# Attention with normalised q and k: q's first transfer is issued by ScalarE before its first table load instead of after it

## The chip, the cores and the metric

The kernel runs on one core of one Trainium2 chip. The core has five engines that work side by side, each with its own list of instructions: TensorE (PE in the profile; PEld is its weight load), VectorE (DVE), ScalarE (ACT), GpSimd (POOL) and SyncE (SP, which here only issues transfers). SP and ACT both issue DMAs; each engine that issues has a queue of its own, and all queues are served by the same 16 DMA engines. Engines wait for each other, and for transfers, on semaphores. The metric is the device time of one launch in microseconds (us); lower is better.

## The reference

For each of 32 heads, with 2048 positions of 20 numbers each in bf16, the rows of q and k are divided by their norms (plus 1e-6), the logits are scaled by one number `t` per head, and softmax attention is formed:

```
qn = q / (jnp.sqrt((q * q).sum(axis=-1, keepdims=True)) + eps)
kn = k / (jnp.sqrt((k * k).sum(axis=-1, keepdims=True)) + eps)
logits = jnp.einsum('bhqd,bhkd->bhqk', qn, kn) * t[None, :, None, None]
attn = _softmax(logits, axis=-1)
return jnp.einsum('bhqk,bhkd->bhqd', attn, v)
```

The inputs are q, k, v of shape 1 x 32 x 2048 x 20 and `t` of 32 numbers.

## The kernel before

The 32 heads are taken in 8 groups of 4. For a group, q and k are loaded (tile `qk`), squared (`sqs`), summed (`ssum`), turned into inverse norms (`rn`), multiplied and padded to 32 columns per head (`qpad`, `kpad`), and transposed (`qT`, `kT`). For every block of 128 keys by 512 queries PE forms logits in PSUM; their exponentials are taken in two ways. ACT takes them with its Exp table, two blocks to an instruction (line 1053, `pA` from `psA`). DVE and POOL take the other blocks by integer arithmetic on the bits of a float (lines 398 and 411, `dI` and `dS` from `psD`). PE multiplies the results with v (`vaug`), whose extra column of ones gives the softmax denominator.

No engine decides its order at run time. `make_plan` simulates the five engines with costs and latencies written in the source, and puts each operation in its engine's list when it is simulated to start; the instructions are then written out in that order with the semaphore waits that the data needs. At the start of the program some operations are placed by hand with `finish(op, start, cost, lat)`: it writes the start and the end (start plus latency) into the operation and appends it to its engine's list. The list of ACT is then sorted by start.

The start of the first group matters here. Only the first 4 of its 16 rows per partition are fetched first: the k part by SP, the q part by ACT, each 128 partitions x 4 heads x 80 numbers (80 KB), line 464. Behind k's first part SP issues `t` (tile `tb16`, line 618), the rest of k, the rest of q, and v. ACT's list starts with a dummy activation on `act_scr` (line 611) for which a table load for the square root is put in front of it; it waits for a memset on DVE (line 592). ACT squares k's first part itself (line 377), DVE squares q's (line 376) and sums both (line 378, q's first). ACT takes the two square roots (line 379), and behind the second loads the table for the exponential (line 639). DVE goes on to inverse norms (lines 380, 381, 384) and to `qpad` and `kpad` (line 389).

Between the sums and the norms DVE finds the largest `|t|` into `tmx` (line 619, the operation `flag`). The program exists in two complete plans, and every engine reads `tmx` and takes a branch (lines 1491 and 1492) to one of them. PE does so right after its first 10 warming matmuls (line 666); so its small transposing matmuls (line 677, with more warming ones of line 684 between them), which give `qT` and `kT` for the first logits, come behind the branch. The first logits are at line 849, and fillers that keep PE busy are at line 662.

Of the kernel before, what the change touches and what calls it, by code (L numbers as in the profile page):

```python
# [161 lines left out]
def bass_standalone__qk_norm__prompt_kernel(  # L162
# [15 lines left out]
    with ExitStack() as es:  # L178
# [236 lines left out]
        def part_op(hg, c):  # L415
            b = hg % 2
            f = lambda tl: tl[b][:, :, :, :].rearrange("p h r d -> p (h r d)")
            return dve("vh", NH * R * VW, R4, lambda e: e.tensor_single_scalar(f(vpart[c]), f(vaug), c, ALU.mult),
                       [("v", b, hh) for hh in range(NH)] + [("vz", b)], [("vh", b, c)])
# [29 lines left out]
        def load_qk(hg, a, part=None):  # L449
            b = hg % 2  # L450
            r0, r1 = (0, R) if part is None else PARTS[part]
            if a == 0 and hg == HG - 1:

                ops = []
                for x in range(4):
                    s_ = q[0, hg * NH:(hg + 1) * NH].rearrange("h (i x r) d -> x i h (r d)", x=4, r=R)[x]
                    d_ = qk[b][32 * x:32 * x + 32, a, :, :, :].rearrange("p h r d -> p h (r d)")
                    keys = [("qk", b, a, 0), ("qk", b, a, 1)]
                    ops.append(dma("ldq", lambda e, d=d_, s=s_: e.dma_start(d, s), keys if x else [], [("qkx", b, x)] if x else keys, 0.5, 4.0))
                return ops  # L460
            src = (q, k)[a][0, hg * NH:(hg + 1) * NH].rearrange("h (p r) d -> p h r d", p=128)[:, :, r0:r1, :]
            s_ = src.rearrange("p h r d -> p h (r d)")
            d_ = qk[b][:, a, :, r0:r1, :].rearrange("p h r d -> p h (r d)")
            return [dma("ld" + "qk"[a], lambda e: e.dma_start(d_, s_), [],
                        [("qk", b, a, i) for i in ((0, 1) if part is None else (part,))],
                        0.5, 4.0 if part != 0 else LOAD0)]
# [10 lines left out]
        def tr_op(hg, which, r0, r1):  # L477
            b = hg % 2
            pad, T = (kpad, kT) if which == "k" else (qpad, qT)
            src = pad[b][:, r0:r1, :, :].rearrange("p r h d -> p (r h d)")  # L480
            dst = T[b][:, r0 * 128:r1 * 128].rearrange("p (r n) -> p r n", n=128)
            keys = [(which + "T", b, r) for r in range(r0, r1)]
            o = dma("T" + which, lambda e: e.dma_start_transpose(dst, src),
                       [(which + "pad", b, r) for r in range(r0, r1)], keys, 0.58 + 0.17 * (r1 - r0), TRL + 0.17 * (r1 - r0) + TRK * (hg == 0 and which == "k"))
            o.info = hg
            return o
# [19 lines left out]
        def make_plan(share):  # L506
# [56 lines left out]
            def finish(op, start, cost, lat):  # L563
                op.start, op.done = start, start + lat
                P.put(op)
# [24 lines left out]
            o = P.link(Op("DVE", "z", lambda e: e.memset(zt[:, :], 0.0), [], ["zt"], 0.25, 0.3))  # L590
            finish(o, 0.15, o.cost, o.lat)
            o = P.link(Op("DVE", "z", lambda e: e.memset(act_scr[:, :], 1.0), [], ["scr"], 0.1, 0.15))
# [9 lines left out]
            for b in (1, 2, 3):  # L602
# [8 lines left out]
            o = P.link(Op("ACT", "tab", lambda e: e.activation(act_scr[:, 0:16], act_scr[:, 0:16], ACT.Sqrt),  # L611
                          ["scr"], ["scr0"], 1.5, 1.6))
# [11 lines left out]
            want_sp(load_qk(0, 1, 0)[0])  # L624
            o = P.link(load_qk(0, 0, 0)[0])
            o.eng = "ACT"
            finish(o, 0.8, o.cost, o.lat)
            P.order["ACT"].sort(key=lambda o: o.start)
            t_load()
            for a in (1, 0):  # L630
# [34 lines left out]
            o = Op("PE", "heat", None, ["zt"], [("psA", 0), ("psD", OB(0))])  # L665
# [41 lines left out]
            for r0, r1, a0, a1 in ((4, 16, 1, 2), (4, 16, 0, 1)):  # L707
# [13 lines left out]
                for w_ in ("q", "k")[a0:a1][::-1]:  # L721
                    for c0, c1 in ((8, r1) if w_ == "k" else (r0, r1),):
                        o = tr_op(0, w_, c0, c1)
# [5 lines left out]
            if share:  # L729
                for c in vpart:  # L730
                    o = part_op(0, c)
# [675 lines left out]
            while left:  # L1407
                progressed = False
                for e in P.order:
                    while pos[e] < len(P.order[e]):  # L1410
                        o = P.order[e][pos[e]]
# [29 lines left out]


        plans = [make_plan(True), make_plan(False)]
        n_flag = max(o.cnt for o in plans[0][0].order["DVE"] if o.name == "flag")
        cut = {}
# [109 lines left out]
```

## Time and profile before

| what | us |
|---|---|
| median of 3 runs | 587.89 |
| lowest and highest of them | 587.89, 589.05 |
| the profiled execution's own time | 588.97 |
| its span, first to last instruction | 587.2 |
| ACT busy in the span | 576.7 |
| PE busy in the span | 577.3 |
| DVE busy in the span | 576.1 |
| ACT's first exponential starts at | 9.81 |

Times inside the profile count from the start of the span. An instruction row has its start, its duration, the engine, the line, the operation and the tiles written and read; in square brackets stands how long the engine was idle before it and what ended that. A row with an engine's name and a q (ACTq, SPq) is the sequencer of that engine, which issues transfers; its duration is that of the issue, not of the transfer. For transfers the time "to landing" counts from the start of the issue to the last signal on the semaphore.

### The profile page before, as it was taken

Reading aid. Unit: us, or ns where it says so; the run is one execution under the profiler, and the core shown is the slowest. Engines: PE = TensorE matmul, PEld = TensorE weight load, DVE = VectorE, ACT = ScalarE, POOL = GpSimd, SP = SyncE. Lnnn points to the kernel's source line nnn. Section 1 sums busy time; section 2 is a strip of 40 time slices with the busy share of each in tenths; the row PEclk is TensorE's granted clock in tenths of the full one; section 3 lists DMA queues with packets and bytes.
Section 4 is the critical chain, followed back from the end, with each engine's and each line's share of the span. In section 5 each row is a group of like instructions: output and inputs, shape, how many; then the busy total and the mean of one; then the engine's idle time right before and its main releaser. Section 6 shows DMA issues by size and latency. Waiting matters only on the chain.

```text
span 587.2 us, 16438 instructions
## 1 busy us (share of the span) xinstructions
PE 577.3 (98%) x6799; PEld 164.4 (28%) x6799; DVE 576.1 (98%) x1040; ACT 576.7 (98%) x632; POOL 498.2 (85%) x924
## 2 busy tenths in 40 slices
PE   8999999999999999999999999999999999999997
PEld 4332222322223222232222322222222322222221
DVE  7999999999999999999999999999999999999996
ACT  6999999999999999999999999999999999999996
POOL 2587898897988899788898889888989789999995
PEclk9999999999999999999999999999999999999999
DMA  5640605205051131410523113430054401101000
GB/s 68 102 58 1 118 2 45 48 2 117 5 68 22 39 81 10 60 23 19 102 17 60 17 37 84 31 61 2 1 103 40 68 2 37 38 3 23 7 8 17
DMA packets 132144, 24.19 MB, mean 41 GB/s; under 512 B 121312, under 2 KB 132064, under 8 KB 132064
## 3 DMA queue, kind: packets, MB, share of 16 engines
q1 hardware_dynamic: 131264, 22.96, 25.5%
q8 instruction: 55, 0.90, 0.6%
q10 hardware_dynamic: 800, 0.12, 0.1%
q14 instruction: 25, 0.20, 0.1%
HBM read 7.87 MB, written 2.62 MB: 18 GB/s over the span
## 4 chain that ended last, share of the span: by engine, by line
ACT 90%; PE 6%; DVE 3%; DMA 1%; issue 0%; DVEq 0%
ACT pA L1053 90%; PE psD L871 3%; PE psA L849 2%; DMA qk<-in_q_dram 1%; DVE ssum L301 0%; DVE dI L398 0%; PE psD L849 0%; PE psA L684 0%; DVE rn L329 0%; DVE sqs L298 0%; DVE ssum L378 0%; PE psD L677 0%; DVE accT L423 0%; DVE kT L718 0%; DVE rsb L323 0%
## 5 line engine op out<-in xcount | busy, mean ns | idle before, releaser
L1053 ACT ACTIVATE pA<-psA 128x1024 f16<-128x1024 f32 (+1 forms) x624 | 572.4, 1180 | 1.3 <-PE psA L849 1.1
L411 POOL INT64_ADD dS<-dI x907 | 492.1, 558 | 69.3 <-DVE ost L438 15.7
L398 DVE TENSOR_SCALAR dI<-psD 128x512 int16<-128x512 f32 (+1 forms) x785 | 490.6, 688 | 1.0 <-PE psD L849 0.4
L849 PE MATMUL psA<-qT,kT 32*128 32x512 bf16 x1248 | 245.0, 385 | 1.9 <-ACT pA L1053 0.4
L849 PE MATMUL psD<-qT,kT 32*128 32x512 bf16 x801 | 244.5, 383 | 0.8 <-DVE dI L398 0.6
L871 PE MATMUL psD<-dS,vaug 128*22 128x512 f16 x1600 | 210.2, 383 | 0.0
L871 PE MATMUL psD<-pA,vaug 128*22 128x512 f16 (+1 forms) x1248 | 183.7, 383 | 0.1
L871 PE MATMUL psD<-dI,vaug 128*22 128x512 f16 x800 | 138.7, 383 | 0.0
L871 PE MATMUL psD<-dI,vhalf 128*22 128x512 f16 x800 | 137.6, 382 | 0.0
L849 PEld LDWEIGHTS psA<-qT,kT 32*128 32x128 bf16 x1248 | 58.6, 91 | 225.9 <-ACT pA L1053 219.7
L849 PEld LDWEIGHTS psD<-qT,kT 32*128 32x128 bf16 x801 | 60.3, 91 | 15.7 <-issue 7.5
L871 PEld LDWEIGHTS psD<-dS,vaug 128*22 128x22 bf16 x1600 | 45.5, 89 | 60.9 <-issue 34.4
L871 PEld LDWEIGHTS psD<-pA,vaug 128*22 128x22 bf16 x1248 | 40.5, 89 | 46.8 <-issue 37.9
L871 PEld LDWEIGHTS psD<-dI,vhalf 128*22 128x22 bf16 x800 | 31.0, 89 | 26.1 <-issue 18.9
L871 PEld LDWEIGHTS psD<-dI,vaug 128*22 128x22 bf16 x800 | 30.9, 89 | 23.4 <-issue 19.8
L423 DVE STREAM_TRANSPOSE accT<-psD 128x512 f32<-128x512 f32 x32 | 22.5, 705 | 2.7 <-PE psD L871 2.7
L438 DVE TENSOR_TENSOR ost<-accT,rec 128x320 bf16<-128x320 f32 x32 | 16.3, 510 | 0.0
L662 PE MATMUL psD<-zt 128*128 128x128 bf16 x130 | 12.9, 228 | 0.0
L271 DVE TENSOR_TENSOR sqs<-qk 128x1280 bf16<-128x1280 bf16 x14 | 11.7, 839 | 0.0
L805 PE MATMUL psD<-ind,sqT 128*128 128x128 bf16 x140 | 11.5, 221 | 0.0
L662 PEld LDWEIGHTS psD<-zt 128*128 128x128 bf16 x130 | 8.1, 101 | 8.4 <-issue 8.4
L805 PEld LDWEIGHTS psD<-ind,sqT 128*128 128x128 bf16 x140 | 7.9, 98 | 4.8 <-issue 3.9
(66 smaller groups left out, 87.6 us busy)
## 6 DMA issues: line engine op xcount, KB each, us to landing
vaug<-in_v_dram SPq DMA_DIRECT2D x32, 80.0 KB, 4.3
qk<-in_k_dram SPq DMA_DIRECT2D x7, 320.0 KB, 3.9
out_dram<-ost SPq DMA_DIRECT2D x28, 80.0 KB, 1.9
qk<-in_q_dram SPq DMA_DIRECT2D x6, 320.0 KB, 4.0
qk<-in_q_dram SPq DMA_DIRECT2D x4, 80.0 KB, 3.5
out_dram<-ost SPq DMA_DIRECT2D x7, 40.0 KB, 2.0
qk<-in_k_dram SPq DMA_DIRECT2D x1, 240.0 KB, 3.9
qk<-in_q_dram SPq DMA_DIRECT2D x1, 240.0 KB, 4.5
```

The costliest lines, as they stand in the source:

```text
L271: ops.append(dve("sq", w_, R2, lambda e, o=sq, x=x3: e.tensor_tensor(o, x, x, ALU.mult), [("qk", b, a, i) for i in parts] + [("qkx", b, i) ...
L398: lambda e: e.tensor_scalar(dst, psD[:, pb * QW:(pb + n) * QW], 1024.0 * LOG2E, 15360.0 - 1024.0 * LOG2K + SHIFTS[0], ALU.mult, ALU.add),
L411: lambda e: e.int64_add(o.bitcast(U64), x.bitcast(U64), add), rd, wr)
L423: return dve("drain", QW, R1, lambda e: e.transpose(accT[:, 16 * b:16 * b + 16, :].rearrange("p b d -> p (b d)"), psO_(sb)), [("psD", OB(s ...
L438: dve("omul", 320 * n, R1, lambda e: e.tensor_tensor(dst, num, rcb, ALU.mult), at + ar, [("ost", hg % 2, g) for g in range(g0, g1)]),
L662: return lambda e: e.matmul(bank, zt[:, 0:128], zt[:, 0:n], start=False, stop=False, skip_group_check=True)
L805: mms = [lambda e, g=g, j=j: e.matmul(dst, sqT[:, (5 * g + j) * 128:(5 * g + j + 1) * 128], ind[:, j, 96 - 32 * g:224 - 32 * g], start=g + ...
L849: return lambda e: e.matmul(dst, lhsT, rhs, tile_position=(32 * hh, 0))
L871: return lambda e: e.matmul(dst, lhsT, rhs, start=first, stop=last, skip_group_check=True, tile_position=(0, 32 * hh))
L1053: a = Op("ACT", "exp", lambda e, s=src, d=dst: e.activation(d, s, ACT.Exp), [("psA", slot)], [("pA", pslot, i) for i in range(WAVES[slot]) ...
```

## The change

The transfer of q's first part gets the planned start 0.0 instead of 0.8, and 0.8 more latency, so its planned end is as before. Since ACT's list is sorted by planned start and the dummy activation stands at 0.6, the transfer now comes first on ACT.

```
@@ make_plan @@
             want_sp(load_qk(0, 1, 0)[0])
             o = P.link(load_qk(0, 0, 0)[0])
             o.eng = "ACT"
-            finish(o, 0.8, o.cost, o.lat)
+            finish(o, 0.0, o.cost, o.lat + 0.8)
             P.order["ACT"].sort(key=lambda o: o.start)
             t_load()
```

This is the head of ACT's list, as a difference from before to now with the semaphore waits; `act_scr` is the dummy activation's scratch tile, and the wait for `s_dma0` is the one for k's first part:

```order
 L1516 UNCONDITIONAL_BRANCH [waits barrier_Pool_Activation_PE_DVE_SP_release]
+L464 DMA qk<-in_q_dram 128x4x80
 L611 ACT_TABLE_LOAD
 L611 ACTIVATE act_scr<-act_scr 128x16 [waits s_dve]
-L464 DMA qk<-in_q_dram 128x4x80
 L377 ACTIVATE sqs<-qk 128x320 [waits s_dma0]
 L379 ACTIVATE nr<-ssum 128x16 [waits s_dve] x2
```

The issue of q's first transfer moved up past the table load and past the dummy activation with its wait for DVE. The lists of PE, DVE, POOL and SP are the same as before, with the same waits.

More of the change, by code (lines that the diff above doesn't have):

```diff
@@ L626, in make_plan @@
             o.eng = "ACT"
-            finish(o, 0.8, o.cost, o.lat)
+            finish(o, 0.0, o.cost, o.lat + 0.8)
             P.order["ACT"].sort(key=lambda o: o.start)
```

## Prediction

> **What bounds the kernel.** I read the page's chain first, then its groups, then the chain in order of time. The page says that nearly all of the span is one chain on ACT:
>
> ```profile
> ACT pA L1053 90%; PE psD L871 3%; PE psA L849 2%; DMA qk<-in_q_dram 1%; DVE ssum L301 0%; DVE dI L398 0%; PE psD L849 0%; PE psA L684 0%; DVE rn L329 0%; DVE sqs L298 0%; DVE ssum L378 0%; PE psD L677 0%; DVE accT L423 0%; DVE kT L718 0%; DVE rsb L323 0%
> L1053 ACT ACTIVATE pA<-psA 128x1024 f16<-128x1024 f32 (+1 forms) x624 | 572.4, 1180 | 1.3 <-PE psA L849 1.1
> ```
>
> The 624 exponentials of line 1053 cover 572.4 us, and ACT has 1.3 us of idle time in front of them, 1.1 of it before the first. So the end is the start of the first exponential plus a dense stream: whatever brings that start and the stream's inputs earlier by one amount brings the end earlier by the same. The chain in order of time says what the first exponential hangs on:
>
> ```profile
> 1.28 3.46 DMA qk<-in_q_dram
> 4.76 0.34 DVE sqs L376
> ...
> 5.12 0.88 DVE ssum L378 x2
> 6.00 0.09 DVE tmx L619
> ...
> 7.13 0.50 PE psA L684 x3
> ...
> 22.95 526.43 ACT pA L1053 x574
> ```
>
> From 1.28 to 4.74 the whole program waits for q's first 80 KB. Behind it come DVE's square, sums and norms, PE's small matmuls, and at last ACT, which heads the chain from 22.95 on. Of the opening stage this transfer is by far the longest piece.
>
> **The issue, moved.** The first rows of the timeline on ACT, on SP and on DVE:
>
> ```profile
> 0.80 0.47 SPq L464 DMA_DIRECT2D qk<-in_k_dram  x1
> 0.81 1.28 ACT L611 ACT_TABLE_LOAD   x1 [0.81 <-PEq L1540]
> 1.16 0.09 DVE L592 MEMSET act_scr<- 128x32 f32 x1
> 1.28 0.46 ACTq L464 DMA_DIRECT2D qk<-in_q_dram  x1
> 1.34 0.48 SPq L618 DMA_DIRECT2D tb<-in_t_dram  x1
> 2.10 0.22 ACT L611 ACTIVATE act_scr<-act_scr 128x16 f32<-128x16 f32 x1
> 3.00 0.47 ACT L377 ACTIVATE sqs<-qk 128x320 bf16<-128x320 bf16 x1 [0.68 <-DMA qk<-in_k_dram]
> 3.11 0.29 DVE L609 TENSOR_TENSOR idn<-idn,accT 128x128 bf16<-128x128 bf16 x1
> 5.12 0.88 DVE L378 TENSOR_REDUCE ssum<-sqs 128x16 f32<-128x320 bf16 x2
> 5.91 0.18 DVE L619 TENSOR_REDUCE tmx<-tb 128x1 f32<-128x32 bf16 x1
> ```
>
> The table load does not itself hold the issue: it runs until 2.09, and the issue starts at 1.28. What held it is the dummy activation's wait for the memset, which ends at 1.25; the sequencer goes on when that wait is met, though the activation itself runs only at 2.10. Now the issue can start when SP's first does, at 0.80. Gain at the issue: 1.28 - 0.80 = 0.48 us.
>
> In return the table load starts after the issue, at about 0.80 + 0.48 = 1.28, ends at 2.56, and the dummy activation at 2.78. k's square began at 3.00, when k landed; 0.22 us of cover are left, and behind them more: its result is needed by the second sum only, about 0.4 us after the first has begun. I cost it at nothing. Were k to land early, the worst would be a square at 2.78, which is still earlier than before.
>
> **The transfer itself.** The larger term is what the transfer meets. Issues and landings (copies, KB, us to landing), then packets of each queue in three stretches, 1.90 to 2.40 (first line), 2.40 to 2.90 (the next two) and 2.90 to 3.50 (the last two); q1 is SP's queue, q10 ACT's:
>
> ```profile
> qk<-in_q_dram ACTq DMA_DIRECT2D x1, 80.0 KB, 3.5
> qk<-in_k_dram SPq DMA_DIRECT2D x1, 80.0 KB, 2.2
> tb<-in_t_dram SPq DMA_DIRECT2D x1, 8.0 KB, 3.2
> ...
> DMA packets 347, 0.06 MB, mean 110 GB/s; under 512 B 347, under 2 KB 347, under 8 KB 347
> ...
> q10 hardware_dynamic: 230, 0.04, 52.5%
> q1 hardware_dynamic: 218, 0.03, 35.5%
> ...
> q10 hardware_dynamic: 85, 0.01, 17.3%
> q1 hardware_dynamic: 43, 0.00, 14.9%
> ```
>
> The same 80 KB take 2.2 us for k and 3.46 for q. q's packets ran well until 2.90 (230 in 0.5 us), and then came to a crawl: 85 in the next 0.6 us, with only 43 of SP's, so the engines were not full but held up. That begins when k's packets are through and `t` follows on SP's queue: 8 KB that take 3.2 us, which speaks for `t` as the thing that crawls, and q's packets behind it on the same engines.
>
> Issued at 0.80, q shares the engines with k instead, and k's packets stand ahead of `t` in SP's queue. Upper and lower end of q's landing: alone it would take k's 2.2 us, 3.0; with the old 3.46 us, 4.26. Between them: k alone landed at 3.0; 512 more packets of q (80 KB in rows of 160 bytes), at 448 per 0.5 us as in the second stretch, add 0.57; but the first stretch, with 347, had room for some 100 of them (0.11 us). An estimate from these rows is 3.0 + 0.57 - 0.11 = 3.46. I take it, since it lies nearer to the row for k, whose company it now has. That is 4.74 - 3.46 = 1.28 us earlier.
>
> Two covers stand close behind. DVE's set-up ends at 3.11 + 0.29 = 3.40: no landing before that is worth more than 1.34. And `tmx` (5.91) needs `t`, which lands at 1.34 + 3.2 = 4.54; shifted by 1.28 it would start at 4.63. That holds if `t` lands no later than now. It starts later, as k's packets end later (up to 0.46), but without q's beside it. I take these two as equal; the bounds are a landing at 4.54 (limit 1.35) and at 5.00 (limit 0.89).
>
> **What must come along.** PE's small matmuls come after PE's branch on `tmx`, so they shift with it. Of things that do not shift, the later loads are the ones to look at:
>
> ```profile
> 2.36 0.51 SPq L464 DMA_DIRECT2D qk<-in_q_dram  x1
> DMA to landing us min/median/max: 2.2/3.7/4.5
> ...
> 8.65 0.48 DVE L298 TENSOR_TENSOR sqs<-qk 128x640 bf16<-128x640 bf16 x1
> ...
> 12.00:14.80 2.80, 2.80 (x34) 1.72 (x32) 2.59 (x10) 2.80 (x4) 0.09 (x1) 1.00 0.01 3
> 14.97 0.40 PE L871 MATMUL psD<-pA,vaug 128*22 128x512 bf16 x4
> ```
>
> The rest of k and of q has landed by 2.36 + 4.5 = 6.9, and its first use is at 8.65. The DMA share from 12.00 to 14.80 is 0.01, so v is in by about 12, and its first use at 14.97 may come 2.9 us earlier. The warming matmuls of PE are the next to look at:
>
> ```profile
> 1.66 4.05 PE L666 MATMUL psA<-zt 128*128 128x512 bf16 x9
> 8.06 0.31 PE L677 MATMUL psD<-idn,kpad 128*128 128x128 bf16 x1
> 8.17 0.74 PE L684 MATMUL psA<-zt 128*128 128x128 bf16 x5
> 9.16 0.61 PE L849 MATMUL psA<-qT,kT 32*128 32x512 bf16 x4
> 9.71 1.52 PE L662 MATMUL psD<-zt 128*128 128x128 bf16 x16
> 11.16 0.39 PE L849 MATMUL psA<-qT,kT 32*128 32x512 bf16 x2
> 11.48 0.62 PE L662 MATMUL psD<-zt 128*128 128x128 bf16 x8
> ...
> L662 PE MATMUL psD<-zt 128*128 128x128 bf16 x130 | 12.9, 228 | 0.0
> ...
> 9.81 6.52 ACT L1053 ACTIVATE pA<-psA 128x1024 bf16<-128x1024 f32 x7 [1.12 <-PE psA L849]
> ```
>
> Line 666 ends at 5.71; the next matmul would stand at 7.13 - 1.28 = 5.85, so this does not bind.
>
> **Sum.** 0.48 at the issue and 0.80 in the transfer, together 1.28; everything else 0. The profiled execution took 588.97 us for a span of 587.2, and lies 1.08 above the median. Against it the sum gives 587.69; against the median 587.89 it gives 586.61, which is my number: 0.22% faster. A measurement of this kernel tells about 0.2% (1.18 us) from no change, so the forecast is at the edge of it.
>
> **Rivals.** First, the transfer takes its 3.46 us wherever it starts: 0.48 is all, 587.41, no measurable change. For it speaks that the crawl's cause is inferred; against it that k's same 80 KB took 2.2. The Trainium skill, in "DMA: Bandwidth & Descriptors", section "Issuing engines are not separate DMA queues", says that transfers from several engines run on the same 16 DMA engines, and that issuing on several saves only the sequencer's time. By that rule this is the outcome; no row contradicts the shared engines, and the packets of q10 and q1 side by side agree with it.
>
> Second, `t` takes over as the last input: q's extra 1.26 us (3.46 - 2.2) go to `t` in part. With a landing at 5.0 to 5.5 the gain is 0.89 to 0.39, 587.0 to 587.5.
>
> Third, more than the shift. One small matmul at 8.17 takes (0.74 - 0.31) / 4 = 0.108 us; one of the 8 at 11.48 takes (0.62 - 0.23) / 7 = 0.056, with 228 ns as the length of a single one. PE still works at about half pace until somewhere in the 16 of 9.71, though line 666 kept it busy from 1.26 to 5.71. If the shorter gap, 5.71 to 5.85 instead of to 7.13, brings the full pace earlier, the 18 small matmuls from 7.13 to 9.24 save up to 18 x 0.052 (0.108 - 0.056) = 0.94; DVE's padding and copies take half of it, so 0.5: 586.1. The Trainium skill, in "TensorE: Matmul & The Clock Gate", Part 1, says that full clock follows a busy window of about 3.4 us, and that the windows run free of the kernel's start. By that rule a nearly closed gap makes this likelier in some executions than others; the 4.4 us of line 666 without full pace show that one such stretch need not do.
>
> Fourth, slower: full pace stays away longer. At half pace a pair of logits and its 8 fillers take 8 x 0.108 + about 0.4 (the pair at 11.16 takes 0.39) = 1.3 us, where now 0.87 pass from 11.16 to the next pair and an exponential needs 0.91 ((6.52 - 1.08) / 6); each exponential in that regime loses 0.4. If full pace comes at the old 10.6 only, the third exponential loses about 0.3 of the gain. It becomes a loss from some 3 exponentials later, at about 14 us, and one of over 0.2% (2.46 / 0.4, 6 exponentials) at about 17: 589.1. Against it: before, the pace was full by 11.2, and PE is now busy earlier.
>
> **Chances.** Forecast 0.50 (of it 0.38 beyond 0.2%, 0.12 within), transfer as long as ever 0.10, `t` last 0.13, earlier full pace 0.17, slower 0.10. Faster is 0.38 + 0.17 = 0.55; same 0.12 + 0.10 + 0.13 = 0.35; slower 0.10. The range runs from a bit below the third rival, 585.9, to the case in which nearly all of the gain goes, 587.8; the likeliest case's own is 586.5 to 587.0.
>
> **What would show it.** In the profile of the changed kernel ACTq's issue stands at 0.80, the table load at about 1.28; q lands near 3.5 and DVE's square (line 376) starts there instead of at 4.76; `tmx` starts near 4.63 without a wait for `t`; PE's first small matmul is at 5.85 and the first exponential at 8.53. A square of q near 4.3 shows the first rival, idle time before `tmx` the second, small matmuls spaced by about 0.056 the third, gaps between the first exponentials the fourth. The forecast is wrong if the first exponential moves up and the last does not.

## The result, and the profile after

The changed kernel takes 587.11 us in the median of 9 runs (586.90 to 587.39); the kernel before, run beside it, 588.86 (587.89 to 589.30, 9 runs). The ratio is 0.9975, with a 95% interval of 0.9965 to 0.9985: 0.25% faster, some 1.5 us. The median of before is 1 us above the 587.89 that the three first runs gave; why its runs lie so far apart is taken up in the experiments, which explain part of it.

The span of the profiled execution went from 587.2 to 585.6, its own time from 588.97 to 587.36. The page of the profile still has the same stream, with the start moved; first the span, then the exponentials as a group and the chain by line:

```profile
span 585.6 us, 16438 instructions
...
ACT pA L1053 90%; PE psD L871 3%; PE psA L849 2%; PE psA L666 1%; DVE ssum L301 0%; DVE dI L398 0%; PE psD L849 0%; DVE sqs L298 0%; DVE rn L329 0%; DVE accT L423 0%; PE psA L684 0%; DVE kpad L345 0%; PE psD L666 0%; DVE kT L718 0%; DVE qpad L345 0%
...
L1053 ACT ACTIVATE pA<-psA 128x1024 f16<-128x1024 f32 (+1 forms) x624 | 572.4, 1178 | 0.9 <-PE psA L849 0.7
```

The stream is as long as before, 572.4 us. q's transfer is gone from the chain; the warming matmuls of line 666, of which the prediction said only that they do not bind, stand in its place. In order of time the chain now begins so:

```profile
1.87 3.84 PE psA L666 x9
5.71 0.16 issue
5.87 0.50 PE psA L684 x3
6.37 0.21 PE psD L677 x2
6.58 0.21 PE psA L684 x2
6.79 0.27 PE psD L677 x3
7.06 0.02 issue
7.08 0.29 ACT kT L694
```

PE is busy until 5.71 and goes on at 5.87; a gap of 1.4 us has become one of 0.16. That the chain names the warming does not make it a bound: in a run below, in which it ends 1.3 us earlier, PE goes on at 5.87 all the same. The opening rows of the timeline, and the first transfers with their us to landing:

```profile
0.81 0.49 ACTq L464 DMA_DIRECT2D qk<-in_q_dram  x1
1.35 1.28 ACT L611 ACT_TABLE_LOAD   x1 [1.35 <-PEq L1540]
2.64 0.21 ACT L611 ACTIVATE act_scr<-act_scr 128x16 f32<-128x16 f32 x1
3.30 0.47 ACT L377 ACTIVATE sqs<-qk 128x320 bf16<-128x320 bf16 x1 [0.45 <-DMA qk<-in_k_dram]
3.49 0.33 DVE L376 TENSOR_TENSOR sqs<-qk 128x320 bf16<-128x320 bf16 x1
4.64 0.17 DVE L619 TENSOR_REDUCE tmx<-tb 128x1 f32<-128x32 bf16 x1
6.80 0.25 PE L677 MATMUL psD<-idn,kpad 128*128 128x128 bf16 x1
6.88 0.44 PE L684 MATMUL psA<-zt 128*128 128x128 bf16 x5
7.60 0.40 PE L849 MATMUL psA<-qT,kT 32*128 32x512 bf16 x4
8.03 8.36 ACT L1053 ACTIVATE pA<-psA 128x1024 bf16<-128x1024 f32 x9 [0.67 <-PE psA L849]
```

```profile
qk<-in_k_dram SPq DMA_DIRECT2D x1, 80.0 KB, 2.5
qk<-in_q_dram ACTq DMA_DIRECT2D x1, 80.0 KB, 2.6
tb<-in_t_dram SPq DMA_DIRECT2D x1, 8.0 KB, 2.9
```

q is issued 0.47 us earlier and its transfer takes 2.6 in place of 3.5; DVE's square starts at 3.49 instead of 4.76. k's first part takes 0.3 longer in q's company; ACT's square of k waits for it (3.30 instead of 3.00), but that square is needed only by the second sum, so nothing on the way to the first exponential does. `t` takes 0.3 less. The first exponential moved by more than q did: from 9.81 to 8.03, which is 1.78, of which 1.27 came with the square. The other 0.51 lie in PE's small matmuls: the five at 6.88 take 0.44 together, where those of before took 0.74, so that from the first small matmul to the first logits there are 7.60 - 5.87 = 1.73 us instead of 9.16 - 7.13 = 2.03, and the first logits take 0.40 instead of 0.61. That PE reached its full pace earlier is thus worth 0.30 + 0.21 = 0.51 in this execution. (Half pace is the 0.108 us per small matmul that the prediction reads from the profile before, full pace the 0.056.)

### The profile page after: what moved, and what is told of

It reads as the page before. It is cut to its first block, busy times and chain, and to the rows that moved or that the text cites. A ratio compares the mean times of both kernels' runs of the same rounds, so it can differ in the third digit from the quotient of the medians.

```text
span 585.6 us, 16438 instructions
## 1 busy us (share of the span) xinstructions
PE 576.6 (98%) x6799; PEld 163.9 (28%) x6799; DVE 575.9 (98%) x1040; ACT 576.8 (99%) x632; POOL 499.9 (85%) x924
## 4 chain that ended last, share of the span: by engine, by line
ACT 90%; PE 7%; DVE 2%; issue 0%; DVEq 0%
ACT pA L1053 90%; PE psD L871 3%; PE psA L849 2%; PE psA L666 1%; DVE ssum L301 0%; DVE dI L398 0%; PE psD L849 0%; DVE sqs L298 0%; DVE rn L329 0%; DVE accT L423 0%; PE psA L684 0%; DVE kpad L345 0%; PE psD L666 0%; DVE kT L718 0%; DVE qpad L345 0%
## 5 line engine op out<-in xcount | busy, mean ns | idle before, releaser
L1053 ACT ACTIVATE pA<-psA 128x1024 f16<-128x1024 f32 (+1 forms) x624 | 572.4, 1178 | 0.9 <-PE psA L849 0.7
```

The lines of the kernel that those rows point to most:

```text
L1053: a = Op("ACT", "exp", lambda e, s=src, d=dst: e.activation(d, s, ACT.Exp), [("psA", slot)], [("pA", pslot, i) for i in range(WAVES[slot]) ...
```

## The experiments

All have the kernel before beside them on the same chip; its median there was 588.64 to 588.95. In the edits, `...` stands for the part of a line that stays.

**Was it the table load, or the wait behind it?** The order is left as it was, and the dummy activation is made to wait for nothing (it reads a constant, its scratch column is taken out of the memset, and the dependence on `scr` is dropped):

```
-... e.memset(act_scr[:, :], 1.0) ...
+... e.memset(act_scr[:, 16:32], 1.0) ...
-... e.activation(act_scr[:, 0:16], act_scr[:, 0:16], ACT.Sqrt), ["scr"], ...
+... e.activation(act_scr[:, 0:1], nc.const_aps.scalar_like(1.0, act_scr[:, 0:1]), ACT.Sqrt), [], ...
```

> The kernel before, with ScalarE's list in its old order, but the dummy activation reads a constant and so waits for nothing. Theory (the dummy activation's wait for VectorE held the issue, not the table load): the issue of q's first transfer starts by 0.90 us, while the table load still runs, q lands at about 3.5, and the time is that of the changed kernel, 587.1 us, ratio about 0.997. Rival (the table load itself stands in the way): the issue stays at 1.28 or goes to 2.1, and the time stays near 588.9, ratio 1.000 or above.

Measured: 587.05 us (587.00 to 587.49), ratio 0.9970 (0.9958 to 0.9982). The timeline of this kernel:

```profile
0.81 1.28 ACT L611 ACT_TABLE_LOAD   x1 [0.81 <-PEq L1540]
0.88 0.47 ACTq L464 DMA_DIRECT2D qk<-in_q_dram  x1
3.42 0.32 DVE L376 TENSOR_TENSOR sqs<-qk 128x320 bf16<-128x320 bf16 x1 [0.32 <-DMA qk<-in_q_dram]
```

The issue starts at 0.88 with the table load in front of it and still running until 2.09. So the table load did not hold the transfer; the wait for the memset did, and taking that wait away gives all that the change gives.

**Does the gap on PE matter by itself?** The kernel before, with three more warming matmuls that fill the gap:

```
-... for i in range(HEAT0 - 1)]
+... for i in range(12)]
```

> The kernel before with 13 warming matmuls of line 666 in place of 10, so that TensorE has hardly a gap between 1.26 and the branch; q is not touched. Theory (part of the gain is that the shorter gap lets TensorE reach its full pace earlier): q still lands near 4.74 and the first small matmul stays near 7.13, but the full pace begins by about 8 us, not at 10.7, the first exponential starts at about 9.3 instead of 9.81, and the time falls by about 0.5 against the profiled execution of before, with the nine times of before between 587.9 and 589.3 replaced by times at the low end. Rival (only q's landing matters): the first exponential stays at 9.8 and the times scatter as before.

Measured: 588.28 us (588.11 to 588.52, 11 runs), ratio 0.9988 (0.9979 to 0.9997). Its timeline:

```profile
1.67 4.62 PE L666 MATMUL psA<-zt 128*128 128x512 bf16 x12
4.85 0.32 DVE L376 TENSOR_TENSOR sqs<-qk 128x320 bf16<-128x320 bf16 x1 [1.44 <-DMA qk<-in_q_dram]
7.24 0.34 PE L684 MATMUL psA<-zt 128*128 128x128 bf16 x3 [0.95 <-DVE qpad L389]
7.80 0.44 PE L684 MATMUL psA<-zt 128*128 128x128 bf16 x5
8.95 1.94 ACT L1053 ACTIVATE pA<-psA 128x1024 bf16<-128x1024 f32 x2 [0.67 <-PE psA L849]
```

q lands as late as ever, and PE's first small matmul stands 0.1 later than before; yet the first exponential comes 0.86 earlier, since all of PE's small matmuls run at full pace. The 12 warming ones take 4.62 us, less than 12 at the old spacing, so that the pace changed among them. The runs lie within 0.41 us, those of before on the same chip between 587.80 and 590.47 (28 runs). In the median the filled gap is worth 0.65. The runs did not come to stand at the low end of those of before, as was expected: all lie above its lowest by 0.3 or more. So PE's pace accounts for part of the scatter of before, and the rest is not explained here.

**And the other way round?** The changed kernel with three warming matmuls fewer, which opens the gap again:

```
-... for i in range(HEAT0 - 1)]
+... for i in range(6)]
```

> The changed kernel with 7 warming matmuls of line 666 in place of 10: they end at about 4.4, so that the gap before the first small matmul (5.86) is again about 1.4 us, as in the kernel before. Theory (shift 1.28 from q, about 0.5 from the earlier full pace): q lands at 3.46 as in the changed kernel, the full pace begins later than 6.84 (about 10 us), the first exponential starts at 8.5 to 8.6 rather than 8.03, and the time is 0.5 or more above the changed kernel's 587.1, so about 587.6. Rival (the gap does not matter): 8.03 and 587.1 as in the changed kernel.

Measured: 587.67 us (586.86 to 588.29, 11 runs), ratio 0.9979 (0.9969 to 0.9989). The profiled execution took 588.07:

```profile
3.49 0.33 DVE L376 TENSOR_TENSOR sqs<-qk 128x320 bf16<-128x320 bf16 x1
5.87 0.49 PE L684 MATMUL psA<-zt 128*128 128x128 bf16 x3 [1.44 <-DVE qpad L389]
6.90 0.74 PE L684 MATMUL psA<-zt 128*128 128x128 bf16 x5
8.44 1.89 PE L662 MATMUL psD<-zt 128*128 128x128 bf16 x16
8.54 1.94 ACT L1053 ACTIVATE pA<-psA 128x1024 bf16<-128x1024 f32 x2 [1.12 <-PE psA L849]
10.76 2.86 ACT L1053 ACTIVATE pA<-psA 128x1024 f16<-128x1024 f32 x3 [0.28 <-PE psA L849]
```

q's part is as in the changed kernel, to the hundredth. PE's small matmuls are at half pace, and the first exponential is at 8.54: 1.27 before 9.81, the shift alone. And the price of the prediction's fourth rival shows: the 16 fillers take 1.89 at half pace, the third exponential waits for its logits and starts at 10.76. In a dense row one exponential starts 0.92 us after the other (three take 2.86, two 1.94), so that the third could have started at 8.54 + 1.84 = 10.38; some 0.4 of the gain goes. With the gap open the runs scatter over 1.4 us again; the lowest are as fast as the changed kernel. So the gap does not set the pace: it leaves it to chance. The time alone would not tell this run from the changed kernel (their intervals overlap); the profile does. It shows as well that the warming does not bind: it ends 1.3 us earlier here, and PE's first small matmul stands at 5.87 as in the changed kernel.

**Why did q's transfer shrink?** Two runs leave q's issue at 1.28 and change only `t`'s transfer. In the first its 128 rows of 64 bytes come from 128 places of v, so the logits are scaled by other numbers. In the second there are 16 rows, to a tile of their own (`tdum`) that nobody reads, and a memset fills `tb16` with ones:

```
-src = bass.AP(t.tensor, 0, [[0, 128], [1, H]])
+src = bass.AP(v.tensor, 0, [[5120, 128], [1, H]])
```

> The kernel before, but the 128 rows of 64 bytes that fill the tile of t come from 128 different places of v instead of 128 times from the 64 bytes of t, so the logits are scaled by other numbers; issue, packets and sizes are the same. Theory (the 128 reads of one address make t crawl, and q's packets behind it): t lands in well under 3.2 us after its issue, q (issued at 1.28 as before) lands at 3.6 to 3.9 instead of 4.74, and about 0.9 to 1.1 us come off the start of the first exponential. Rival (small packets of any kind, or the company of two queues, make the crawl): q lands near 4.7 and the time is that of before.

```
-src = bass.AP(t.tensor, 0, [[0, 128], [1, H]])
+src = bass.AP(t.tensor, 0, [[0, 16], [1, H]])
-... e.dma_start(tb16[:, :], src) ...
+... e.dma_start(tdum[0:16, :], src) ...
+... e.memset(tb16[:, :], 1.0) ...
```

> The kernel before, but t's transfer has 16 rows of 64 bytes in place of 128, into a tile that nobody reads; the tile of t is filled with ones by a memset on VectorE, so the scale of the logits is left out. Issues, order and waits are as before. Theory (t's 128 small packets are what q's packets were held up by, the one address being only part of it): q, issued at 1.28 as before, lands at about 3.7 (its own 2.2 us, some sharing with k's last packets and with the rest of k), and VectorE's square starts there; 0.9 to 1.1 us come off the first exponential, more if the shorter gap brings TensorE's full pace earlier. Rival (the crawl is not t's: any second queue has it, or the rest of k makes it): q lands at 4.3 or later.

The issues of the two kernels, us to landing, of the one with 128 places first, and the square of the one with 16 rows:

```profile
qk<-in_q_dram ACTq DMA_DIRECT2D x1, 80.0 KB, 3.1
tb<-in_v_dram SPq DMA_DIRECT2D x1, 8.0 KB, 2.8
```

```profile
qk<-in_q_dram ACTq DMA_DIRECT2D x1, 80.0 KB, 2.6
tdum<-in_t_dram SPq DMA_DIRECT2D x1, 1.0 KB, 2.3
```

```profile
3.91 0.33 DVE L376 TENSOR_TENSOR sqs<-qk 128x320 bf16<-128x320 bf16 x1 [0.50 <-DMA qk<-in_q_dram]
```

Their times are 587.54 us (ratio 0.9980, 0.9970 to 0.9989) and 587.53 (0.9980, 0.9971 to 0.9990). The first expectation was met by less than half: with 128 places q takes 3.1, not the 2.3 to 2.6 that were expected; the single address accounts for some 0.4 of the excess. The second holds nearly: with 16 rows q's square starts at 3.91 (3.7 was expected), and q takes 2.6, as in the changed kernel, at the old issue time. So `t`'s 128 small packets did hold q's back, by about 0.85 in all (3.46 less 2.6), and about half of it comes with the one address. Each share rests on one profile, and the same transfer at the same issue differed by 0.1 to 0.3 between other pairs of profiles here, so the halves are rough. Why 64-byte packets from different places do so too stays open.

The times of these two runs gained more than q's landing, 1.4 us in the median. Their profiled executions show where from: PE was at full pace from the first small matmul. With 128 places the first exponential came 1.36 earlier (8.45), of which 0.40 came with the square; with 16 rows 1.81 (8.00), of which 0.85. What `t`'s packets cost is therefore read from the transfer, not from the time.

**How early is early enough?** The kernel before with DVE's first two memsets exchanged, so that the dummy activation's wait ends earlier:

```
-            o = P.link(Op("DVE", "z", lambda e: e.memset(zt[:, :], 0.0), [], ["zt"], 0.25, 0.3))
+            o = P.link(Op("DVE", "z", lambda e: e.memset(act_scr[:, :], 1.0), [], ["scr"], 0.1, 0.4))
             finish(o, 0.15, o.cost, o.lat)
-            o = P.link(Op("DVE", "z", lambda e: e.memset(act_scr[:, :], 1.0), [], ["scr"], 0.1, 0.15))
+            o = P.link(Op("DVE", "z", lambda e: e.memset(zt[:, :], 0.0), [], ["zt"], 0.25, 0.05))
             finish(o, 0.4, o.cost, o.lat)
```

> The kernel before with VectorE's first two memsets exchanged, so that the dummy activation's wait ends about 0.2 us earlier; the issue of q's first transfer should start at about 1.05, between 1.28 and 0.81. Theory (the earlier the issue, the more of q's packets pass before t's): q's time in transit shrinks as well, to between 2.65 and 3.46, about 3.05, so that it lands at about 4.1. Rival (a transfer's time does not depend on when it is issued, until both first transfers start together): transit 3.46, landing 4.5.

Measured: 586.90 us (586.73 to 587.26), ratio 0.9970 (0.9958 to 0.9982).

```profile
1.01 0.44 ACTq L464 DMA_DIRECT2D qk<-in_q_dram  x1
3.43 0.33 DVE L376 TENSOR_TENSOR sqs<-qk 128x320 bf16<-128x320 bf16 x1
```

Issued at 1.01, q lands at 3.4, in 2.4 us, less than the 2.6 in the changed kernel, perhaps because it shares less of its time with k. Both theories named 4.1 or later, and both were wrong: 0.27 us of issue were worth 1.33 of start, and a steady shrinking of the transfer would have given less. Somewhere between an issue at 1.01 and one at 1.28, then, `t` catches q; no run lies between the two.

**What bounds next?** The changed kernel with `t` cut to 16 rows, run once:

> The changed kernel with t's transfer cut to 16 rows as in the run with 16 rows on the kernel before, and the tile of t filled with ones. Theory (behind q's landing the next bound is VectorE's set-up, which ends at 3.41): q lands by 3.3, the square starts at 3.4 to 3.5 and no earlier, since VectorE is then the later one, and the first exponential is within 0.15 us of the changed kernel's 8.03 for the same onset of TensorE's full pace. Rival (q's packets beside k's are the bound also without t): landing and square stay at 3.46 and 3.49.

Measured: 586.77 us; q takes 2.6 as in the changed kernel, lands at 3.4, and the square starts at 3.43 instead of 3.49. Theory and rival lie close together here. With `t` cut q landed hardly earlier, not by 3.3, so the rival is nearer: q's packets beside k's are a bound also without `t`. DVE's set-up ends at 3.40, at the same moment within 0.1, so a further gain would need both to be earlier. The first exponential was at 7.52, 0.5 earlier than in the changed kernel's first profile; all of PE's small matmuls were at full pace here, which the expectation had set aside.

**Can it be improved?** The warming matmuls among PE's small ones cut to one at each of three places, on the changed kernel; then the same on the kernel with the exchanged memsets, beside the changed kernel once more:

```
-op.info = [lambda e: e.matmul(psA[:, 3 * QW:3 * QW + 128], zt[:, 0:128], zt[:, 0:128])] * n
+op.info = [lambda e: e.matmul(psA[:, 3 * QW:3 * QW + 128], zt[:, 0:128], zt[:, 0:128])]
```

> The changed kernel with one warming matmul of line 684 at each of three places, in place of 3, 2 and 5: a version that might beat both. Theory (these 7 matmuls stand on the way to the first exponential, each 0.108 us at half pace and 0.056 at full pace, and VectorE's padding covers part of them): the first exponential starts 0.2 to 0.5 earlier than 8.03, and the time is 586.6 to 586.9. Rival (they are needed for the early full pace, or wholly covered by VectorE and ScalarE): the full pace begins later or nothing moves, 587.1 or above.

> The kernel before with VectorE's first two memsets exchanged (issue of q's first transfer at 1.01 with the table load still in front of it) and with one warming matmul of line 684 at each place in place of 3, 2 and 5. If both gains add: q lands at 3.4, the first exponential starts 0.3 earlier than with the exchange alone for the same onset of full pace, and the time is 586.4 to 586.7, below the changed kernel on the same chip by 0.4 or more. If the shorter way to the first exponential is taken up by the next thing (VectorE's padding, ScalarE's second table load): 586.8 or above.

> The changed kernel once more, beside the one with both edits on the same chip: 587.1, ratio to before 0.9975 within its interval, and q landing at 3.4 to 3.5 as in the first run of it.

Measured: 586.77 (586.67 to 587.02, ratio 0.9966, 0.9954 to 0.9978) for the first, 586.90 (586.67 to 587.01, ratio 0.9968, 0.9957 to 0.9979) for the second, and 586.89 (586.78 to 587.25, ratio 0.9970, 0.9959 to 0.9980) for the changed kernel beside it. The gains do not add, and none of these is clearly faster than the changed kernel. Rows of the three in this order say why:

```profile
7.69 2.86 ACT L1053 ACTIVATE pA<-psA 128x1024 bf16<-128x1024 f32 x3 [0.61 <-PE psA L849]
```

```profile
3.73 0.33 DVE L376 TENSOR_TENSOR sqs<-qk 128x320 bf16<-128x320 bf16 x1 [0.33 <-DMA qk<-in_q_dram]
7.29 0.40 PE L849 MATMUL psA<-qT,kT 32*128 32x512 bf16 x4 [0.19 <-DVE qT L697]
```

```profile
3.46 0.33 DVE L376 TENSOR_TENSOR sqs<-qk 128x320 bf16<-128x320 bf16 x1
6.40 0.44 PE L684 MATMUL psA<-zt 128*128 128x128 bf16 x5
7.55 2.86 ACT L1053 ACTIVATE pA<-psA 128x1024 bf16<-128x1024 f32 x3 [0.67 <-PE psA L849]
```

The first had half pace through its small matmuls and is 0.34 ahead of the changed kernel's first profile (8.03), as expected. But at full pace the edit saves hardly anything: from q's square to the first exponential (7.72) the second kernel takes 3.99 us, where the changed kernel in this second profile, with all of its small matmuls at full pace, takes 4.09 (3.46 to 7.55) without the edit. With fewer warming matmuls the first logits wait for DVE's copy of `qT` instead. In the second kernel q landed 0.3 later than with the exchange alone, at the same issue; 1.01 may be close to the point at which `t` catches it.

## Why the prediction was right, and where it was off

- **The issue.** Predicted at 0.80, seen at 0.81. That the dummy activation's wait and not the table load held it is shown by the run without that wait.
- **The table load behind it.** Costed at nothing: it ended at 2.63, the dummy activation at 2.85, and k's square waited for k, which landed 0.3 later. Right.
- **The transfer.** The estimate for q's landing was 3.46; the square started at 3.49, and `tmx`, put near 4.63, at 4.64. That it fits to the hundredth is luck: the estimate gave the stretch from 1.90 to 2.40 some 100 packets more than the 347 of before and the next one the old 448; in the changed kernel the first carried 324 and the second 678, and the two errors cancel. The cause, `t`'s packets, was inferred and is now shown, by the run with 16 rows. The company of k cost k 0.3, inside the 0.46 allowed.
- **`t` as the next bound.** Taken as neither earlier nor later; it came 0.3 earlier, and was no bound.
- **The first rival, by which only the issue's time is saved.** That the DMA engines are shared held: k's transfer was longer by 0.3. That only the issue's 0.47 is saved did not: 1.27 was. What this rival leaves out is that an earlier issue changes whom a transfer meets.
- **The step that was off: "everything else 0".** The first exponential was put at 8.53 and came at 8.03. This is the third rival, with its sign (the five at 6.88 are about 0.05 apart): it was held to be an alternative, at 0.17, but the shift itself closes the gap, and PE's pace follows. The run that opens the gap shows both terms apart: 8.54, the shift alone. That the rival's 0.5 meets the 0.51 of the profile is luck. Its working took 0.94 at most and let DVE's padding and copies cover half of it. But from q's square to the first exponential there are 5.05 us at half pace throughout (before, and the run with the gap opened), 4.54 in the changed kernel's first profile, where the small matmuls ran at half pace until about 6.8, and 4.09 or 4.10 at full pace throughout (the changed kernel's second profile, and before with the gap filled). So the pace is worth up to 0.96: 0.75 before the first logits (2.03 us of before against 7.12 - 5.84 = 1.28 in the changed kernel's second profile), of which the working would have left 0.5, and 0.21 in these logits, which it did not count.
- **The fourth rival** did not happen in the changed kernel, but its mechanism is real: in the run with the open gap the third exponential lost about 0.4 (about 0.3 was worked out).
- **The sum.** Against the profiled execution 587.69 was predicted; it took 587.36. The difference is the 0.51 of PE's pace less 0.18 that was given back. Of that, 0.07 lie between the first exponential and DVE's last multiplication, by the chain's last rows of before and of after below (1.78 earlier at the first exponential, 1.71 here); the rest lies behind it.

```profile
583.89 0.49 DVE ost L438
```

```profile
582.18 0.49 DVE ost L438
```

- **The base.** The 586.61 was counted from 587.89. The changed kernel's 587.11 is 0.5 above it, but the ratio is 0.9975, where 0.9978 was forecast: three runs of before, of which two were 587.89, stood at the low end of its scatter. Against the 588.86 beside the changed kernel the same 1.28 gives 587.58, and the remaining 0.47 is about what PE's pace was worth in the profile. So a base that was too low and a term that was left out cancel in part. The time lies within the stated range, and 0.11 above the 586.5 to 587.0 that was given for the likeliest case. That PE's pace is part of what makes executions of before differ follows from the runs with the filled and the opened gap; no second profile of before shows it in before itself.

## What to carry to other kernels

When a transfer at the start bounds everything, look at what stands ahead of its issue on the issuing engine: here it was the semaphore wait of an unimportant instruction that cost, not the long operation beside it. Look also at whom the transfer will share the DMA engines with: here 128 packets of 64 bytes beside it cost more (0.85 us) than the delay of the issue itself (0.47). And look whether PE's warming ends before its first real work: here closing that gap made the time both lower (by 0.65) and steadier (588.11 to 588.52, where before had 587.80 to 590.47).

## What the runs showed of the hardware

- 128 rows of 64 bytes (8 KB in all) from one address, issued 0.06 us after 80 KB on another queue, lengthened that 80 KB transfer from 2.6 us (16 such rows) to 3.5; from 128 places to 3.1.
- The moment of PE's full pace varies between executions that warm up alike. With the same 10 matmuls of line 666 ending near 5.7 or a little before, the small matmuls of the kernel before were still at 0.108 us each at 8.17 in its profile; in the run with t's rows from v, also with a gap of a microsecond, they were at full pace from the first (the second row below, three in 0.34 where before has 0.50). The Trainium skill, in "TensorE: Matmul & The Clock Gate", Part 1, says that the activity windows of about 3.4 us run free of the kernel's start, so that the same warming can fall well or badly; the runs agree with that, though the windows themselves were not seen. The half microsecond that the Trainium skill gives there for this variation is too little here: the changed kernel with 16 rows of `t` reached full pace within its warming (the last row below, 3.28 where the others have 4.05), while before had warmed for 4.45 us without a gap (1.26 to 5.71) and still had half pace.
- The row of granted clock on the page of the profile shows 9 from the first slice on, in the half-pace stretch too; the pace had to be read from the spacing of the matmuls.

The run with `t`'s rows from v, timeline, and the warming of the changed kernel with 16 rows of `t`:

```profile
1.67 4.05 PE L666 MATMUL psA<-zt 128*128 128x512 bf16 x9
6.75 0.34 PE L684 MATMUL psA<-zt 128*128 128x128 bf16 x3 [1.03 <-DVE qpad L389]
...
1.66 3.28 PE L666 MATMUL psA<-zt 128*128 128x512 bf16 x9
```
